# Softmax attention for one query row, forward and backward: the twelve middle head pairs load K in two pieces around V, finish dK before V's phase, and walk V by quarters of its rows

## The chip, the cores and the metric

The kernel runs on one core of a Trainium2 chip. The metric is device time in microseconds (us). A core has TensorE (PE in the profile, its weight loads PEld), VectorE (DVE), ScalarE (ACT), GpSimd (POOL) and SyncE (SP). The first four compute; SP here does nothing but issue transfers, on one queue. Matmuls write to PSUM, everything else lives in SBUF, and q, k, v and the outputs lie in HBM, which is reached by DMA: sixteen DMA engines serve the core.

## The reference

There are 32 heads, one query row each, 8192 keys and a head size of 128, all in bf16. The forward function is softmax attention, and the gradients of q, k and v are asked for too.

```python
B, H, Sq, Skv, Dh = 1, 32, 1, 8192, 128

def _fwd_reference(q, k, v):
    scale = q.shape[-1] ** -0.5
    scores = jnp.einsum('bhqd,bhkd->bhqk', q, k) * scale
    attn = _softmax(scores, axis=-1)
    return jnp.einsum('bhqk,bhkd->bhqd', attn, v)

_out, _vjp = jax.vjp(_f, q, k, v)
_grads = _vjp(grad_out)          # dq, dk, dv
```

For one head with the probabilities p, this is out = p·V, dV = p ⊗ grad_out, dp = V·grad_out, ds = p·(dp − sum(p·dp))·scale, dq = ds·K, dK = ds ⊗ q. K and V are each read once (67 MB each) and dK and dV are each written once (67 MB each). That makes 268 MB in all, and hardly any arithmetic beside it.

## The kernel before, in words

**Tiles.** Two heads make one turn t, and there are 16 turns. A turn's K is one SBUF tile of 128 partitions by 128 rows by 128 columns (4 MB; partition p holds 128 consecutive rows of the pair), and so is its V. Three K tiles and two V tiles rotate: K of turn t+2 goes into the tile of turn t−1, V of turn t+2 into that of turn t. dK and dV are written over K and V in place, eight blocks of 16 rows each, by one VectorE product per block (`outer`, L366), and stored from there (`store`, L376). So a load into a tile waits until the store out of it has landed.

**Scores.** `k_block(t, c)` (L197) transposes block c of K on VectorE (L200) into one of three buffers of the pool `XK`, and four matmuls (L208) add the block's scores into the PSUM bank `s_ps`. `s_back` transposes the bank, `s_top` finds the maximum, `s_exp` and `s_sum` give the exponentials and their sum, `p_of` (L246) gives p, four times repeated for the products, and the weights `win_p`.

**V's phase.** Three things read V before dV overwrites it. `contract(t, "p")` (L344, 32 matmuls) gives the output. dp comes from two halves in turns 3 to 14 (`wide(t)`): half of the rows go through TensorE transposes and ScalarE copies (`v_part`, L272 and L278) and `v_scores` (L289); the other half goes through VectorE transposes (`v_block`, L296, which also uses the `XK` buffers) and `v_wide` (L306). Both halves add into the bank `dp_ps`. `v_back` (L315) transposes it, `pd_sum` (L324) sums, `ds_of` (L329 to L335) gives ds, and `contract(t, "ds")` gives dq.

**Order.** The order on each engine is written out by hand: between L100 and L590 nothing is reordered, so the program's order is each engine's order. In a middle turn before the change, VectorE does five dK products of the turn before (`dk(0, 5)`), then the softmax, then the four V blocks with three more dK products spread among them, then two dV products, `v_back`, one dV product, `ds_of`, and then five dV products alternating with the K blocks 0 to 4 of the next turn, followed by K blocks 5 to 7.

**SP's queue.** It is in order: a transfer that has to wait holds those behind it. In a turn it issues the store of dK(t−1), the store of dV(t), the load of K(t+2) (waiting for the landing of the dK(t−1) store) and the load of V(t+2) (waiting for the landing of the dV(t) store).

Turns 0 to 2 and 15 use another order (`first()` and the `else` branches), with V wholly on TensorE and ScalarE. Turn 14 stores dK in two pieces, turn 15 dK and dV in four.

Of the kernel before, what the change touches and what calls it, by code (L numbers as in the profile page):

```python
# [21 lines left out]
ST = 4  # L22
K_BUFS = 3
V_BUFS = 2


@with_exitstack
def kernel(
# [49 lines left out]
    def load(x, X, t, parts):  # L78
        L = NT // parts
        for c in range(parts):  # L80
            nc.sync.dma_start(X[t][:, c * L:(c + 1) * L, :], rows_of(x, t, c * L, (c + 1) * L))
# [3 lines left out]

    def load_v(t, parts=1):
        load(v, Vt, t, parts)

    rows = consts.tile([H, 2, D], BF16)
    nc.scalar.dma_start(rows[:, 0, :], q.rearrange("b h s d -> (b h s) d"))  # L90
# [81 lines left out]
    dq_all = consts.tile([P, H], F32)  # L172

    def prepare(t):
        x = st[t] = {}
        x["m"] = psM.tile([P, 512], F32, tag="m", name="m_ps")
        for s in range(2):
            nc.tensor.matmul(x["m"][s * HF:(s + 1) * HF, 256:512],
                             lhsT=ident[0:H, 2 * t + s:2 * t + s + 1].to_broadcast([H, HF]),
                             rhs=rows[:].rearrange("h a d -> h (a d)"), start=True, stop=True, skip_group_check=True)  # L180
        x["qd"] = small.tile([P, 2, D], BF16, tag="qd", name="qd")
        nc.scalar.copy(x["qd"][:].rearrange("p a d -> p (a d)"), x["m"][:, 256:512])
# [12 lines left out]
            nc.scalar.copy(do_wide[a * QD:(a + 1) * QD, :, a * QD + SL - 1], do_four[a * QD:(a + 1) * QD, :, t])  # L195

    def k_block(t, c):  # L197
        x = st[t]
        X = xkpool.tile([P, BN, NW, QD], F32, tag="XK", name="XK_sb")
        nc.vector.transpose(X[:], Kt[t][:, c * BN:(c + 1) * BN, :].rearrange("p n d -> p (n d)").bitcast(F32).rearrange(  # L200
            "p (n w j) -> p n w j", n=BN, w=NW))
        if c == 0:
            x["s"] = psS.tile([P, 512], F32, tag="s", name="s_ps")
        cols = X[:].rearrange("p n w i -> p (n w i)").bitcast(BF16).rearrange(
            "p (n w i e) -> p w e n i", n=BN, w=NW, e=2)
        for w in range(NW):
            for e2 in range(2):
                nc.tensor.matmul(x["s"][:], lhsT=q_win[:, 2 * w + e2, SL - 1 - c:SL - 1 - c + P],  # L208
                                 rhs=cols[:, w, e2], start=(c == 0 and w == 0 and e2 == 0),
                                 stop=(c == NB - 1 and w == NW - 1 and e2 == 1), skip_group_check=True)  # L210
# [45 lines left out]
    def wide(t):  # L256
        return 3 <= t < HP - 1
# [22 lines left out]
    def v_scores(t, z):  # L280
        x = st[t]
        cols = x.pop(("XV", z)).rearrange("p m s -> p (m s)").bitcast(BF16).rearrange(
            "p (m s e) -> p e m s", s=P, e=2)
        if z == 0:
            x["dp"] = psD.tile([P, 512], F32, tag="dp", name="dp_ps")
        at = SL - 2 - 2 * z
        for e2 in range(2):
            for b in range(NQ):
                nc.tensor.matmul(x["dp"][b * QD:(b + 1) * QD, :], lhsT=do_win[:, b // 2, e2, at:at + QD],  # L289
                                 rhs=cols[:, e2, :, b * QD:(b + 1) * QD],  # L290
                                 start=(z == 0 and e2 == 0), stop=(not wide(t) and z == NZ - 1 and e2 == 1), skip_group_check=True)

    def v_block(t, r):

# [5 lines left out]
    def v_wide(t, r):  # L300
        cols = st[t].pop(("XW", r))[:].rearrange("p n w i -> p (n w i)").bitcast(BF16).rearrange(
            "p (n w i e) -> p w e n i", n=NM, w=NW, e=2)
        at = SL - 1 - (SL // 2 + r)
        for w in range(NW):
            for e2 in range(2):
                nc.tensor.matmul(st[t]["dp"][:], lhsT=do_wide[:, 2 * w + e2, at:at + P], rhs=cols[:, w, e2], start=False,  # L306
                                 stop=(r == SL // 2 - 1 and w == NW - 1 and e2 == 1), skip_group_check=True)

    def rows_in(x):
        return x.rearrange("p (m r) -> p m r", r=SL)  # L310
# [40 lines left out]
    def gather(t, which):  # L351
        S_ = backs.tile([P, 4, D], F32, tag="back", name="S_" + which)
        nc.scalar.copy(S_[:].rearrange("p j d -> p (j d)"), acc.pop(which)[:])
        bank, to = st[max(st)]["m"], (o_all if which == "p" else dq_all)
        pick = lane[:].rearrange("p (w j) -> p j w", j=4)
        at = 8 if which == "p" else 16
        for j in range(4):
            nc.tensor.matmul(bank[:, at:at + 2 * ST], lhsT=S_[:, j, :], rhs=pick[:, j, :],
                             start=(j == 0), stop=(j == 3), skip_group_check=True)
        nc.scalar.copy(to[:, 2 * (t - ST + 1):2 * (t + 1)], bank[:, at:at + 2 * ST])  # L360
# [104 lines left out]
    for t in range(1, HP + 1):  # L465
        o = t - 1
        now = t < HP
        parts = 4 if o == HP - 1 else 2 if o == HP - 2 else 1

        def dk(a, b):  # L470
            for r in range(a, b):
                outer(o, "ds", r)
                if (r + 1) % (NB // parts) == 0:
                    store(o, "ds", parts, r * parts // NB)

        blocks = now and wide(t)

        if blocks:

            dk(0, 5)  # L480
            s_back(t)
            s_top(t)
            for m in range(3):
                v_bank(t, m)
            v_block(t, 0)
            rs = s_exp(t)
            for m in range(3):
                v_copy(t, m)
            v_block(t, 1)
            v_part(t, 3)  # L490
            s_sum(t, rs)
            v_scores(t, 0)
            v_wide(t, 0)
            dk(5, 6)
            p_of(t)
            v_part(t, 4)
            v_part(t, 5)
            v_block(t, 2)
            v_wide(t, 1)
            v_part(t, 6)  # L500
            v_part(t, 7)
            v_block(t, 3)
            contract(t, "p")
            v_scores(t, 1)
            v_wide(t, 2)
            v_wide(t, 3)
            weights_do(t + 1)
            if wide(t + 1):
                weights_wide(t + 1)
        else:  # L510
            dk(0, 3)
            if now:
                v_part(t, 3)
                v_part(t, 4)
                s_back(t)
                s_top(t)
                v_scores(t, 0)
                v_part(t, 5)
                v_part(t, 6)
                rs = s_exp(t)  # L520
                for m in (7, 8, 9):
                    v_bank(t, m)
                s_sum(t, rs)
                v_copy(t, 7)
                v_copy(t, 8)
            dk(3, 4)
            if now:
                p_of(t)
                v_copy(t, 9)
                v_scores(t, 1)  # L530
                v_part(t, 10)
                v_part(t, 11)
                contract(t, "p")
                v_part(t, 12)
                v_part(t, 13)
                v_scores(t, 2)
                v_part(t, 14)
                v_part(t, 15)
                v_scores(t, 3)
                if t + 1 < HP:  # L540
                    weights_do(t + 1)
                    if wide(t + 1):
                        weights_wide(t + 1)
        if not now:
            dk(4, NB - 1)
            results()
            dk(NB - 1, NB)
            break
        dk(6 if blocks else 4, NB)
        fine = t == HP - 1  # L550
        outer(t, "p", 0)
        outer(t, "p", 1)
        if fine:
            store(t, "p", 4, 0)
        v_back(t)
        pd_sum(t)
        if t % ST == 0:
            gather(o, "ds")
        outer(t, "p", 2)
        ds_of(t)  # L560
        contract(t, "ds")
        if t % ST == ST - 1:
            gather(t, "p")
        if t + 1 < HP:
            prepare(t + 1)
        else:
            gather(t, "ds")
        for r in range(3, NB):
            outer(t, "p", r)
            if fine and r % 2:  # L570
                store(t, "p", 4, r // 2)
            if t + 1 < HP and t != 1 and r >= HALF - 1:
                k_block(t + 1, r - HALF + 1)
        if not fine:
            store(t, "p")
        if t == 1:
            for c in range(HALF + 1):
                k_block(t + 1, c)
        if t + 1 < HP:
            for c in range(HALF + 1, NB):  # L580
                k_block(t + 1, c)
                if not wide(t + 1):
                    v_part(t + 1, c - HALF - 1)
            if t + 2 < HP:
                weights_q(t + 2)
        if t + 2 < HP:
            load_k(t + 2)
            load_v(t + 2)

    order.__exit__(None, None, None)  # L590

# [29 lines left out]
```

## Time and profile before

| | |
|---|---|
| median of 3 runs | 635.58 us (635.32 to 635.61) |
| profiled execution | 635.21 us, span 633.4 us |
| moved | 268.92 MB, mean 425 GB/s |
| busy: VectorE | 558.7 us, 88% of the span |
| busy: TensorE matmuls | 426.1 us, 67% |
| busy: ScalarE | 156.9 us, 25% |
| mean granted TensorE clock | 0.83 of full speed |

The profile is one execution. Its first part gives busy time by engine, the second cuts the span into 40 slices of 15.8 us (digits are tenths; the DMA row is the mean busy share of the sixteen DMA engines), the third lists the DMA queues, the fourth follows the chain of work that ended last back from the end. The trace also answers for stretches: who waited for whom, when SP issued what, and the clock that TensorE was granted. Transfers on one queue follow one another, so a transfer's time from issue to landing holds the rest of the transfers before it.

### The profile page before, as it was taken

To read this page: it belongs to the slowest core of one execution; us is meant where nothing else is said; L and a number is where in the kernel's file an instruction comes from. 1 tells how busy PE (TensorE), PEld (TensorE's weight loads), DVE (VectorE), ACT (ScalarE), POOL (GpSimd) and SP (SyncE) were. 2 spreads that over 40 slices of the span, in tenths; PEclk is the share of its full clock that TensorE was granted. 3 is DMA by queue.
4 is the path that set the end of the run, shared out by engine and by line. 5 is a ranking of instruction groups with operands and counts; after the bars stand their busy time and mean duration, and the time that the engine had idled before them with its cause. 6 is when DMAs were issued, how large, how long until landed. Compare 5 with 4: busy or idle time off the path is not lost.

```text
span 633.4 us, 7259 instructions
## 1 busy us (share of the span) xinstructions
PE 426.1 (67%) x2876; PEld 227.8 (36%) x2876; DVE 558.7 (88%) x662; ACT 156.9 (25%) x407; POOL 9.3 (1%) x27
## 2 busy tenths in 40 slices
PE   5968686478665767457776586756758667387950
PEld 2635252243423425134352342524415243152630
DVE  7688988989989899798998979899898998989891
ACT  1616052040311304114041220412304032040610
POOL 2000000000000000000000000000000000000000
PEclk9979597887788887878878888888898788987955
DMA  8999999999999999999999999999999999999996
GB/s 364 431 429 403 447 431 429 430 428 426 436 432 434 433 430 435 429 430 427 429 430 430 432 434 435 432 435 436 426 435 431 432 429 432 426 435 429 416 422 269
DMA packets 12177, 268.92 MB, mean 425 GB/s; under 512 B 1520, under 2 KB 1520, under 8 KB 1520
## 3 DMA queue, kind: packets, MB, share of 16 engines
q1 hardware_dynamic: 12048, 268.46, 98.9%
q8 instruction: 22, 0.36, 0.2%
q14 instruction: 11, 0.09, 0.0%
q10 hardware_dynamic: 96, 0.02, 0.0%
HBM read 134.23 MB, written 134.23 MB: 424 GB/s over the span
## 4 chain that ended last, share of the span: by engine, by line
DMA 42%; DVE 30%; PE 15%; issue 7%; ACT 3%; DVEq 0%; ACTq 0%; SPq 0%
DMA out_dram<-K 22%; DMA K<-in_k_dram 18%; DVE XK_sb L200 12%; DVE K L366 10%; PE T_ps L272 6%; DVE V L366 5%; PE dp_ps L306 3%; PE s_ps L208 2%; ACT XV_sb L278 2%; PE acc_p L344 2%; PE dp_ps L289 1%; DVE sT L215 1%; DMA rows<-in_grad_out_dram 1%; PE m_ps L223 1%; PE acc_ds L344 1%
## 5 line engine op out<-in xcount | busy, mean ns | idle before, releaser
L208 PE MATMUL s_ps<-XK_sb,q_win 128*128 128x512 bf16 x512 | 149.7, 433 | 50.0 <-DVE XK_sb L200 46.8
L200 DVE STREAM_TRANSPOSE XK_sb<-K 128x1024 f32<-128x1024 f32 x128 | 152.4, 1224 | 14.4 <-DMA K<-in_k_dram 12.0
L366 DVE TENSOR_TENSOR V<-p_rep,qd 128x2048 bf16<-128x2048 bf16 x128 | 151.9, 1205 | 2.9 <-ACT K L278 2.4
L366 DVE TENSOR_TENSOR K<-ds_rep,qd 128x2048 bf16<-128x2048 bf16 x128 | 147.8, 1209 | 0.1
L208 PEld LDWEIGHTS <-q_win 128*128 128x128 bf16 x512 | 53.7, 107 | 139.1 <-issue 103.7
L272 PE MATMUL T_ps<-ident_f,V 128*128 128x128 f32 x640 | 102.4, 320 | 0.1
L272 PEld LDWEIGHTS T_ps<-ident_f,V 128*128 128x128 f32 x640 | 91.7, 167 | 14.2 <-issue 2.2
L278 ACT COPY XV_sb<-T_ps 128x512 f32<-128x512 f32 x144 | 78.5, 587 | 69.5 <-PE T_ps L272 69.3
L344 PE MATMUL acc_ds<-K,win_ds 128*32 128x512 bf16 x512 | 50.7, 566 | 28.8 <-ACT win_ds L244 27.3
L296 DVE STREAM_TRANSPOSE XV_blk<-V 128x1024 f32<-128x1024 f32 x48 | 59.6, 1241 | 7.7 <-PE dp_ps L306 7.4
L223 PE MATMUL m_ps<-ident_f,top 128*128 128x128 f32 x16 | 6.5, 405 | 71.9 <-DVE top L222 71.9
L306 PE MATMUL dp_ps<-XV_blk,do_wide 128*128 128x512 bf16 x192 | 49.2, 387 | 0.0
L185 ACT COPY q_win<-q_blk 128x16 bf16<-128x16 bf16 x16 | 4.2, 261 | 159.8 <-PE s_ps L208 159.8
L344 PEld LDWEIGHTS <-win_ds 128*32 128x32 bf16 x512 | 16.3, 126 | 50.5 <-ACT win_ds L244 27.0
L344 PE MATMUL acc_p<-V,win_p 128*32 128x512 bf16 x512 | 30.9, 380 | 1.5 <-ACT win_p L244 1.5
L223 PEld LDWEIGHTS m_ps<-ident_f,top 128*128 128x128 f32 x16 | 2.6, 164 | 78.4 <-issue 73.2
L289 PE MATMUL dp_ps<-XV_sb,do_win 128*32 128x512 bf16 x288 | 24.1, 412 | 8.3 <-ACT XV_sb L278 8.1
L233 ACT ACTIVATE e<-sT,nbias 128x128 f32<-128x128 f32 x16 | 8.3, 520 | 80.7 <-DVE nbias L230 80.7
L306 PEld LDWEIGHTS <-do_wide 128*128 128x128 bf16 x192 | 16.9, 98 | 27.5 <-issue 13.0
L315 DVE STREAM_TRANSPOSE dpT<-dp_ps 128x512 f32<-128x512 f32 x16 | 11.5, 717 | 13.6 <-PE dp_ps L306 12.3
L324 PE MATMUL m_ps<-pd,same 128*128 128x1 f32 x32 | 6.3, 267 | 19.6 <-DVE m_ps L318 19.6
L344 PEld LDWEIGHTS <-win_p 128*32 128x32 bf16 x512 | 12.4, 96 | 14.4 <-issue 4.6
(68 smaller groups left out, 206.7 us busy)
## 6 DMA issues: line engine op xcount, KB each, us to landing
K<-in_k_dram SPq DMA_DIRECT2D x15, 4096.0 KB, 19.3
V<-in_v_dram SPq DMA_DIRECT2D x14, 4096.0 KB, 19.3
out_dram<-K SPq DMA_DIRECT2D x14, 4096.0 KB, 28.2
out_dram<-V SPq DMA_DIRECT2D x14, 4096.0 KB, 20.2
V<-in_v_dram SPq DMA_DIRECT2D x8, 1024.0 KB, 11.3
out_dram<-V SPq DMA_DIRECT2D x8, 1024.0 KB, 19.2
K<-in_k_dram SPq DMA_DIRECT2D x4, 1024.0 KB, 8.0
out_dram<-K SPq DMA_DIRECT2D x2, 2048.0 KB, 13.8
```

What stands on the lines that cost most here:

```text
L200: nc.vector.transpose(X[:], Kt[t][:, c * BN:(c + 1) * BN, :].rearrange("p n d -> p (n d)").bitcast(F32).rearrange("p (n w j) -> p n w j", ...
L208: nc.tensor.matmul(x["s"][:], lhsT=q_win[:, 2 * w + e2, SL - 1 - c:SL - 1 - c + P], rhs=cols[:, w, e2], start=(c == 0 and w == 0 and e2 == 0),
L223: nc.tensor.transpose(x["m"][:, 128:256], top[:].to_broadcast([P, P]), ident_f[:])
L233: nc.scalar.activation(e[:].rearrange("p (c n) -> p n c", c=NB), x["sT"][:, :, 0:NB], ACT.Exp, bias=nbias[:], scale=scale, accum_out=rs[:])
L272: nc.tensor.transpose(T_ps[:, j, :], words[:, at * P:(at + 1) * P], ident_f[:])
L278: nc.scalar.copy(x["XV", z][:, i * TB:(i + 1) * TB, :], x.pop(("T", m))[:])
L289: nc.tensor.matmul(x["dp"][b * QD:(b + 1) * QD, :], lhsT=do_win[:, b // 2, e2, at:at + QD], rhs=cols[:, e2, :, b * QD:(b + 1) * QD], start ...
L296: nc.vector.transpose(X[:], Vt[t][:].rearrange("p n d -> p (n d)").bitcast(F32).rearrange("p (m r w j) -> p m r w j", r=SL, w=NW, j=QD)[:, ...
L306: nc.tensor.matmul(st[t]["dp"][:], lhsT=do_wide[:, 2 * w + e2, at:at + P], rhs=cols[:, w, e2], start=False, stop=(r == SL // 2 - 1 and w = ...
L315: nc.vector.transpose(dpT[:].rearrange("p m r -> p (m r)"), x.pop("dp")[:])
L344: nc.tensor.matmul(acc[which][b * QD:(b + 1) * QD, :], lhsT=win[which][:, g, at:at + QD], rhs=X[:, 4 * g:4 * g + 4, :].rearrange("p n d -> ...
L366: nc.vector.tensor_tensor(X[:, a:b, :].rearrange("p n (a b) -> p n a b", b=R), x[which][:, a:b, :].unsqueeze(2).to_broadcast([P, BN, D // ...
```

## The change

It acts on turns 3 to 14, the ones in which `wide(t)` holds.

- **Loads.** `load_pair` loads the first five of K's eight blocks (`NA = 5`), then V, then the last three blocks of K, as three transfers instead of two. It waits for the same landings as before.
- **K blocks.** Blocks 0 and 1 of turn t+1 come before `v_back(t)`; blocks 2 to 4 at the end of turn t, after the last dV product; blocks 5 to 7 at the start of turn t+1, ahead of the dK products. `weights_q` goes with them.
- **dK.** All eight dK products of turn t−1 come before V's phase: four ahead of `s_back`, one between `s_top` and `s_exp`, three between `s_sum` and `p_of`.
- **V.** Three V blocks are transposed first. Then four quarters follow, each with one `v_wide`, eight matmuls of `contract(t, "p")`, two `v_part`, and the two dV products that overwrite that quarter's rows (blocks 0 to 5 in the first three quarters). `v_scores` comes at the end, the K blocks 0 and 1 of the next turn behind it, then `v_back`; dV products 6 and 7 stand on either side of `ds_of`.
- **dp's bank.** The first `v_wide` opens the sum, the last `v_scores` closes it.

```diff
+    def load_pair(t):
+        cut = NA * BN if wide(t) else NT
+        nc.sync.dma_start(Kt[t][:, 0:cut, :], rows_of(k, t, 0, cut))
+        load_v(t)
+        if cut < NT:
+            nc.sync.dma_start(Kt[t][:, cut:NT, :], rows_of(k, t, cut, NT))
...
         if blocks:
-            dk(0, 5)
+            for c in range(NA, NB):
+                k_block(t, c)
+            weights_q(t + 1)
+            dk(0, 4)
             s_back(t)
             s_top(t)
-            for m in range(3):
-                v_bank(t, m)
-            v_block(t, 0)
+            dk(4, 5)
             rs = s_exp(t)
...
             s_sum(t, rs)
-            v_scores(t, 0)
-            v_wide(t, 0)
-            dk(5, 6)
+            dk(5, NB)
             p_of(t)
...
+            for r in range(3):
+                v_block(t, r)
+            for i in range(4):
+                v_wide(t, i)
+                if i == 0:
+                    v_block(t, 3)
+                contract(t, "p", i * NG // 4, (i + 1) * NG // 4)
+                for z in range(2):
+                    v_part(t, z * (NM // TB) + i)
+                if i < 3:
+                    outer(t, "p", 2 * i)
+                    outer(t, "p", 2 * i + 1)
+            for z in range(2):
+                v_scores(t, z)
             weights_do(t + 1)
             if wide(t + 1):
                 weights_wide(t + 1)
+            k_block(t + 1, 0)
+            k_block(t + 1, 1)
+            early = NB - 2
...
-        dk(6 if blocks else 4, NB)
+        if not blocks:
+            dk(4, NB)
+            outer(t, "p", 0)
+            outer(t, "p", 1)
...
         v_back(t)
         pd_sum(t)
...
-        outer(t, "p", 2)
+        outer(t, "p", early)
         ds_of(t)
         contract(t, "ds")
...
-        for r in range(3, NB):
+        done = 2 if blocks else 0
+        for r in range(early + 1, NB):
             outer(t, "p", r)
...
         if t + 1 < HP:
-            for c in range(HALF + 1, NB):
+            for c in range(done, NA if wide(t + 1) else NB):
                 k_block(t + 1, c)
...
         if t + 2 < HP:
-            load_k(t + 2)
-            load_v(t + 2)
+            load_pair(t + 2)
```

The loads of turns 3 to 14 are issued at the ends of turns 1 to 12. Turn 15 still loads its K whole, but two of its K blocks are asked for in the middle of turn 14.

More of the change, by code (lines that the diff above doesn't have):

```diff
@@ L24 @@
 V_BUFS = 2
+NA = 5
 @with_exitstack
@@ L174, in prepare @@
     def prepare(t):
-        x = st[t] = {}
+        x = st.setdefault(t, {})
         x["m"] = psM.tile([P, 512], F32, tag="m", name="m_ps")
@@ L197, in k_block @@
     def k_block(t, c):
-        x = st[t]
+        x = st.setdefault(t, {})
         X = xkpool.tile([P, BN, NW, QD], F32, tag="XK", name="XK_sb")
@@ L283, in v_scores @@
             "p (m s e) -> p e m s", s=P, e=2)
-        if z == 0:
+        if z == 0 and not wide(t):
             x["dp"] = psD.tile([P, 512], F32, tag="dp", name="dp_ps")
@@ L290, in v_scores @@
                                  rhs=cols[:, e2, :, b * QD:(b + 1) * QD],
-                                 start=(z == 0 and e2 == 0), stop=(not wide(t) and z == NZ - 1 and e2 == 1), skip_group_check=True)
+                                 start=(not wide(t) and z == 0 and e2 == 0),
+                                 stop=(z == (1 if wide(t) else NZ - 1) and e2 == 1), skip_group_check=True)
     def v_block(t, r):
@@ L303, in v_wide @@
         at = SL - 1 - (SL // 2 + r)
+        if r == 0:
+            st[t]["dp"] = psD.tile([P, 512], F32, tag="dp", name="dp_ps")
         for w in range(NW):
             for e2 in range(2):
-                nc.tensor.matmul(st[t]["dp"][:], lhsT=do_wide[:, 2 * w + e2, at:at + P], rhs=cols[:, w, e2], start=False,
-                                 stop=(r == SL // 2 - 1 and w == NW - 1 and e2 == 1), skip_group_check=True)
+                nc.tensor.matmul(st[t]["dp"][:], lhsT=do_wide[:, 2 * w + e2, at:at + P], rhs=cols[:, w, e2],
+                                 start=(r == 0 and w == 0 and e2 == 0), stop=False, skip_group_check=True)
     def rows_in(x):
@@ L353, in gather @@
         nc.scalar.copy(S_[:].rearrange("p j d -> p (j d)"), acc.pop(which)[:])
-        bank, to = st[max(st)]["m"], (o_all if which == "p" else dq_all)
+        bank, to = st[max(u for u in st if "m" in st[u])]["m"], (o_all if which == "p" else dq_all)
         pick = lane[:].rearrange("p (w j) -> p j w", j=4)
@@ L478 @@
         if blocks:
-            dk(0, 5)
+            for c in range(NA, NB):
+                k_block(t, c)
+            weights_q(t + 1)
+            dk(0, 4)
             s_back(t)
             s_top(t)
-            for m in range(3):
-                v_bank(t, m)
-            v_block(t, 0)
+            dk(4, 5)
             rs = s_exp(t)
[L487 to L490, printed above, removed]
             s_sum(t, rs)
-            v_scores(t, 0)
-            v_wide(t, 0)
-            dk(5, 6)
+            dk(5, NB)
             p_of(t)
[L496 to L506, printed above, removed]
+            for r in range(3):
[12 more added lines that the diff above has]
+                v_scores(t, z)
             weights_do(t + 1)
@@ L509 @@
                 weights_wide(t + 1)
+            k_block(t + 1, 0)
+            k_block(t + 1, 1)
+            early = NB - 2
         else:
+            early = 2
             dk(0, 3)
@@ L548 @@
             break
-        dk(6 if blocks else 4, NB)
         fine = t == HP - 1
[L551 to L554, printed above, removed]
+        if not blocks:
+            dk(4, NB)
+            outer(t, "p", 0)
+            outer(t, "p", 1)
+            if fine:
+                store(t, "p", 4, 0)
         v_back(t)
@@ L571 @@
                 store(t, "p", 4, r // 2)
-            if t + 1 < HP and t != 1 and r >= HALF - 1:
-                k_block(t + 1, r - HALF + 1)
+            if not blocks and t + 1 < HP and t != 1:
+                k_block(t + 1, done)
+                done += 1
         if not fine:
             store(t, "p")
-        if t == 1:
-            for c in range(HALF + 1):
+        if t + 1 < HP:
+            for c in range(done, NA if wide(t + 1) else NB):
                 k_block(t + 1, c)
-        if t + 1 < HP:
-            for c in range(HALF + 1, NB):
-                k_block(t + 1, c)
-                if not wide(t + 1):
+                if not wide(t + 1) and c > HALF:
                     v_part(t + 1, c - HALF - 1)
-            if t + 2 < HP:
+            if t + 2 < HP and not wide(t + 1):
                 weights_q(t + 2)
         if t + 2 < HP:
-            load_k(t + 2)
-            load_v(t + 2)
+            load_pair(t + 2)
     order.__exit__(None, None, None)
```

## The prediction, made before the run

> **What bounds the kernel now.** I read the page first: the slices, the queue, the chain.
>
> ```profile
> DMA  8999999999999999999999999999999999999996
> GB/s 364 431 429 403 447 431 429 430 428 426 436 432 434 433 430 435 429 430 427 429 430 430 432 434 435 432 435 436 426 435 431 432 429 432 426 435 429 416 422 269
> ...
> q1 hardware_dynamic: 12048, 268.46, 98.9%
> ...
> DMA 42%; DVE 30%; PE 15%; issue 7%; ACT 3%; DVEq 0%; ACTq 0%; SPq 0%
> ```
>
> The DMA engines are full in 38 of 40 slices; SP's one queue fills 98.9% of their span. The chain, though, gives DVE 30% and PE 15%. It runs through whatever came last at each step, and in a kernel where engines wait for loads and stores wait for engines it can go round either way. So I ask SP when it issued (a middle stretch; start, duration, transfer):
>
> ```profile
> 229.92 0.34 SPq L376 DMA_DIRECT2D out_dram<-V  x1
> 241.73 0.34 SPq L81 DMA_DIRECT2D K<-in_k_dram  x1
> 251.40 0.34 SPq L81 DMA_DIRECT2D V<-in_v_dram  x1
> 251.79 0.42 SPq L376 DMA_DIRECT2D out_dram<-K  x1
> 270.18 0.34 SPq L376 DMA_DIRECT2D out_dram<-V  x1
> 280.45 0.34 SPq L81 DMA_DIRECT2D K<-in_k_dram  x1
> 290.11 0.34 SPq L81 DMA_DIRECT2D V<-in_v_dram  x1
> ```
>
> The K load goes out when the dK store has landed (280.45), the V load when the dV store has (290.11): 9.66 us apart, one 4 MB transfer. The dV store was issued at 270.18, and its turn came at 280.45, 10.3 us later. The dK store waited for nothing but the V load ahead of it on SP. Always at least one transfer lies behind the running one: the queue, not VectorE, sets the pace. The first and last of twelve such K loads were issued at 123.33 and 553.13, so a turn takes 429.8/11 = 39.07 us; four transfers of 4.194 MB at 432 GB/s (below) are 38.84.
>
> VectorE's margin is read from its waits in 100 to 560 us (us, times, longest), about 11.8 turns:
>
> ```profile
> DVE dpT L315 <- PE dp_ps L306: 11.3, 11, 1.4
> DVE XK_sb L200 <- DMA K<-in_k_dram: 11.0, 10, 2.5
> DVE XV_blk L296 <- PE dp_ps L306: 6.6, 11, 1.6
> DVE rinv L249 <- PE m_ps L238: 3.3, 9, 0.4
> ```
>
> VectorE waits 11.0 us for K, 1.0 a turn: it is held by the queue. Without that its own turn would be about 38.1.
>
> **The change, part by part.** The profiled execution took 635.21 us, 1.8 beyond its span of 633.4 and 0.37 below the median 635.58. I add to it and put the same difference on the median.
>
> *Bytes and pieces.* The bytes are the same. Twelve K loads become two transfers each. What a cut costs shows where loads of 1 MB run (5 to 19 us) beside 4 MB ones (245 to 550 us):
>
> ```profile
> DMA packets 858, 5.94 MB, mean 424 GB/s; under 512 B 134, under 2 KB 134, under 8 KB 134
> ...
> DMA packets 4534, 131.69 MB, mean 432 GB/s; under 512 B 506, under 2 KB 506, under 8 KB 506
> ```
>
> 4.194 MB take 9.89 us in four pieces and 9.71 in one: 0.06 us a cut, twelve cuts 0.7 us. Both stretches are full, so this is on the path. The lower end is 0 (the difference may be the two small row loads in the first stretch). The upper end is the row load that stood alone, 8 KB in 3.3 us from issue to landing: twelve of those are 40 us. But the added piece is issued right behind V's load, with up to 9.7 us of bytes before it, as the 1 MB pieces were; I take 0.7.
>
> The Trainium skill (DMA: Bandwidth & Descriptors, Latency and other measured facts) gives about 0.6 us to the first byte on this kind of queue. Paid twelve times this would be 7.2 us, 643.5 in place of 636.3; the rows above show it hidden behind a queued transfer, at 0.06.
>
> *SP's order.* The load of K's first part waits for the same landing as before, V's load too, and the third piece for none. While V's load waits for the dV store's landing, only 5/8 of a K load, 6.1 us, is left in the queue where 9.7 was. SP spends 0.34 us on an issue, so nothing runs dry: 0. Behind V's load stand the third piece and the dK store; the queue still holds 9.7 us of V when they are issued. Cost 0.
>
> *Landings.* With the dV store landing at 251.4, K's first part lands at 257.5 (was 261.0), V at 267.2 (was 270.8), K's last part at 270.8. Blocks 5 to 7 now open a turn, so the wait for K moves there: VectorE starts a turn at 270.8 at the earliest.
>
> *VectorE's turn.* The same operations as before, none added: 425.6 us busy in 95 to 560 us, 35.8 a turn, and small gaps of 0.4 (39.07 less 35.8 less 34.8/11.8 of waits, two smaller ones included). Now the walk, with 1.15 us for a K block and 1.13 for a product back to back, 1.2 for a V block. From the start: three K blocks 3.5, four products 4.5, back and maximum 1.2, a product 1.1, the bias 0.45 (TensorE's transpose of the maximum took 0.45 and has 1.1), three products 3.4 that cover exponential, sum and so `rinv` (0.3 us a turn gone), `p` 0.45: V's phase starts at 14.6. Four V blocks last to 19.5. `v_wide(0)` can start once the first is there, at 15.9. A quarter on TensorE is four wide matmuls, eight of `contract` and eight transposes: 0.88 + 0.48 + 0.87 = 2.2 us at full clock, 1.82 + 0.90 + 1.71 = 4.4 at half, from the groups of four and eight in the chain (288.8 to 290.5 full, 364.6 to 368.2 half) and a quarter of 32 contractions (1.91 and 3.60). VectorE's two products per quarter take 2.3. So at full clock it never waits; at half it does. How long V's phase is at half clock now (columns: stretch, its length, TensorE busy, clock, DMA share, GB/s; transposes begin at 320.6 in one turn, 359.3 in the other):
>
> ```profile
> 320.00:322.00 2.00, 1.67 (x8) 0.50 0.87 377
> 322.00:324.00 2.00, 2.00 (x12) 0.50 0.95 410
> 324.00:326.00 2.00, 1.44 (x14) 0.99 1.22 524
> ...
> 360.00:362.00 2.00, 2.00 (x11) 0.50 0.91 393
> 362.00:364.00 2.00, 1.54 (x13) 0.50 0.95 410
> 364.00:366.00 2.00, 2.00 (x12) 0.50 1.18 508
> 366.00:368.00 2.00, 2.00 (x11) 0.50 0.87 377
> 368.00:370.00 2.00, 2.00 (x13) 0.90 0.99 426
> ```
>
> About 3.5 us in one, 8.9 in the other. With 3.5 the first quarter is through 0.4 us after the last V block, and nothing waits after that. With 8.9 the products wait 0.8 and 2.2. Then two K blocks cover `v_scores`, so the 1.0 wait before `dpT` goes; `pd_sum`, now behind eight score matmuls on TensorE, ends about when product 6 does: 0. After product 7 the K blocks run six in a row at 1.15, while TensorE needs 1.03 for one at full clock; at half (1.7), behind 3.6 of `contract`, it would hold VectorE by up to 2.4 through the three buffers. VectorE's turn: 36.2 + 0.4 = 36.6 at best, 36.2 + 3.0 = 39.2 with the long half clock, 41.6 with both. The mix seen now gives something near 38, below 39.07: hidden behind the queue, with the dV store issued 33 us into the turn (19.5 + six products 6.8 + two K blocks 2.3 + `v_back` 1.2 + two products 2.3 + `ds_of` 0.9), so near 303.8 where its place in the queue comes at 319.2: 15 ahead, where it was 10.
>
> The Trainium skill (TensorE: Matmul & The Clock Gate, Part 1) states that about 3.4 us of sustained work free the clock; by that every turn would be the 36.6 one. The 360 us rows disagree: fully busy, and at half for 8.9.
>
> *The end.* K of turn 15 lands as before plus 0.7, and turn 14 asks for two of its blocks where VectorE has two dV products left rather than five: from 573.5 two K blocks, `v_back`, two products, `ds_of`, six K blocks are 14.4 to 16.5, so dK(14) begins near 588 to 590 against 586.4. The last store piece was issued at 620.99 of 633.4; less 2.5 for its bytes and 3.3 for latency, it had 6.6 us to spare. 1.5 to 3.6 later costs 0. If that cover were gone, it would be paid in full.
>
> Sum: 635.21 + 0.7 = 635.9 for a profiled execution, 636.3 on the median.
>
> **The rivals.**
>
> *TensorE's clock makes VectorE the bound.* For it: V's phase now follows some 11 us with almost no TensorE work, and every dV product waits on that quarter. Against it: V's phase begins at half clock now as well. It decides when the mean turn is over 39.07 + 6.6/11 = 39.7. With 41.6 in every turn: 11 × 2.5 − 6.6 = 21, so 657; with a mean of 40.5, 9 more: 645.
>
> *The added transfers are not hidden.* If each stalls the queue by 0.3 to 0.6 us, 12 × 0.3 = 3.6 to 7.2: 639 to 643. It needs gaps in the queue that the 1 MB pieces do not show.
>
> *Faster.* If the 0.23 us by which a turn exceeds four transfers (39.07 against 38.84) is VectorE being late, the earlier dK and dV products win it back: 12 × 0.23 = 2.8, less 0.7, gives 633.5. It decides if any slice is short for want of an issue; the ten us to spare speak against it, and the 22 instruction fetches on these engines explain the rest better. More is not to be had from a full queue.
>
> **How the numbers follow.** My forecast 0.65, with its own range 635.5 to 637.2 (cuts between 0 and twice their price); the clock 0.20; transfers not hidden 0.09; faster 0.06. The range 635.4 to 641 holds the forecast but for 0.03, a third of the clock's cases and two thirds of the transfers': 0.75 to 0.8. Within 0.2% (1.27 us, about what a measurement here can tell from no change) lies the forecast but for a tenth above 636.85: 0.58. Slower: 0.20 + 0.09 + 0.07 and a little: 0.37; faster 0.05.
>
> **What the profile after would show.** Right: DMA full in the same slices, K's first-part loads 39.1 us apart, the K wait moved to the last part's blocks, dV stores issued about 15 us ahead of need, no `rinv` wait, waits of V's products on `T_ps` below 3 us a turn. Wrong: DMA slices below 9 in the middle, K loads over 39.7 apart, VectorE's waits on `T_ps` or `s_ps` above 3.5 a turn (the clock), or short slices just after V's loads (the pieces).

## The result and the profile after

The changed kernel took 636.56 us (median; 635.56 to 638.34) beside 635.33 us (635.07 to 635.61) for the kernel before: a ratio of 1.0017 [1.0009, 1.0024], 1.23 us slower. That is just within the 0.2% that the prediction called no change, and 0.3 us from its 636.3. The profiled execution took 636.0 us with a span of 634.2, 0.8 more than before's. One thing is new at first sight: the times of the kernel before lie within 0.5 us, those of the changed kernel are spread over 2.8.

The page of the changed kernel, the DMA rows of the 40 slices, the queue and the head of the chain:

```profile
DMA  8999999999999999999999999999999999999997
GB/s 362 432 429 400 447 422 432 437 428 429 427 432 435 435 415 425 433 433 421 412 429 431 430 428 437 434 432 428 426 426 432 429 427 430 431 430 429 422 424 320
...
q1 hardware_dynamic: 13776, 268.46, 99.3%
...
DVE 40%; PE 25%; DMA 24%; issue 5%; ACT 3%; DVEq 0%; SPq 0%; ACTq 0%
```

The DMA engines are as full as before, and SP's queue takes even more of their span (99.3% for 98.9). But full is no longer the same as fast. Slices 6, 15, 19 and 20 moved 422, 415, 421 and 412 GB/s with their digit at 9; before, no slice between the fifth and the last three was under 426. The chain now gives DVE 40% and DMA 24%, where it gave 30 and 42. That looks as if VectorE had become the bound; the experiments show that it has not.

When SP issued, in the same stretch as before (start, duration, transfer; L93 is K's first part, L96 its last):

```profile
241.11 0.34 SPq L93 DMA_DIRECT2D K<-in_k_dram  x1
250.78 0.34 SPq L82 DMA_DIRECT2D V<-in_v_dram  x1
251.17 0.43 SPq L96 DMA_DIRECT2D K<-in_k_dram  x1
251.70 0.38 SPq L388 DMA_DIRECT2D out_dram<-K  x1
265.16 0.35 SPq L388 DMA_DIRECT2D out_dram<-V  x1
280.43 0.34 SPq L93 DMA_DIRECT2D K<-in_k_dram  x1
```

The dV store goes out at 265.16 and its turn in the queue comes at 280.43: 15.3 us ahead of need, where the prediction had 15 and before had 10.3. So the queue does not want for an issue here. Yet the twelve K loads, issued from 123.01 to 554.40, are 39.22 us apart, where before's were 39.07: 11 × 0.15 = 1.65 us over the middle turns.

VectorE's waits between 100 and 560 us (us, times, longest):

```profile
DVE V L378 <- PE T_ps L281: 13.8, 17, 1.1
DVE XK_sb L209 <- PE s_ps L217: 10.5, 9, 2.6
DVE XK_sb L209 <- DMA K<-in_k_dram: 6.0, 4, 2.1
```

The waits before `dpT` and `rinv` are gone and the products of V wait for TensorE's transposes instead, 13.8 us or 1.2 a turn. The second line must not be taken at its word throughout. VectorE's timeline over two turns, with the page's row on K's last parts (the median of the us from issue to landing stands at its end) behind it:

```profile
231.80 3.50 DVE L209 STREAM_TRANSPOSE XK_sb<-K 128x1024 f32<-128x1024 f32 x3 [1.35 <-PE s_ps L217]
235.22 4.59 DVE L378 TENSOR_TENSOR K<-ds_rep,qd 128x2048 bf16<-128x2048 bf16 x4
...
246.48 4.62 DVE L306 STREAM_TRANSPOSE XV_blk<-V 128x1024 f32<-128x1024 f32 x4
251.55 7.18 DVE L378 TENSOR_TENSOR V<-p_rep,qd 128x2048 bf16<-128x2048 bf16 x6 [0.45 <-PE T_ps L281]
...
265.05 3.49 DVE L209 STREAM_TRANSPOSE XK_sb<-K 128x1024 f32<-128x1024 f32 x3
270.78 3.50 DVE L209 STREAM_TRANSPOSE XK_sb<-K 128x1024 f32<-128x1024 f32 x3 [2.23 <-PE s_ps L217]
...
291.18 2.36 DVE L378 TENSOR_TENSOR V<-p_rep,qd 128x2048 bf16<-128x2048 bf16 x2 [1.11 <-PE T_ps L281]
293.87 4.80 DVE L378 TENSOR_TENSOR V<-p_rep,qd 128x2048 bf16<-128x2048 bf16 x4 [0.33 <-PE T_ps L281]
```

```profile
K<-in_k_dram SPq DMA_DIRECT2D x12, 1536.0 KB, 19.2
```

K's last part was issued at 251.17, and 19.2 later is 270.4; the trace's record of this landing says 270.65, and block 5 started at 270.78. This wait of 2.23 us, put down to PE, ended when the load landed, and so did the one of 1.35. Two others, of 2.43 and 2.63 us in other turns, did not: there the load had landed 1.3 and 1.0 us earlier, and TensorE's score matmuls, behind `contract(t, "ds")`, released the buffer last. The other five of the nine waits are TensorE's too, 1.8 us in all. So VectorE waits some 12 us for K, 1.0 a turn as before: it is still held by the queue.

The order came out as the prediction walked it. The turn starts at 231.80, V's phase 14.68 us into it (14.6 was predicted), the dV store 33.4 into it (33).

Last, where the bytes were short: two stretches of the same place in neighbouring turns (start and end, length, busy us of PE, PEld, DVE, ACT and POOL with their counts, PEclk, DMA share, GB/s).

```profile
304.00:309.00 5.00, 4.57 (x42) 2.93 (x42) 4.48 (x4) 0.87 (x3) 0.00 (x0) 0.62 1.06 392
344.00:349.00 5.00, 3.53 (x37) 1.23 (x37) 4.57 (x7) 0.76 (x3) 0.00 (x0) 0.72 1.05 446
```

Both are full. In the first, while K's last part is moved, the engines bring 392 GB/s, in the second 446. In the trace's packet records a packet of that part has 12 KB and normally takes an engine 460 ns; in 5 of the 12 turns 13 to 46 of the 128 packets take clearly longer, up to 1.1 us. The engines are busy all that time (without a packet for 0.04 us of 100 to 560, as a mean of the sixteen), so no view of busy shares shows it.

### The profile page after: what moved, and what is told of

Its sections match the earlier page's. It is cut to its first block, busy times and chain, and to the rows that moved or that the text cites. A ratio compares the mean times of both kernels' runs of the same rounds, so it can differ in the third digit from the quotient of the medians.

```text
span 634.2 us, 7269 instructions
## 1 busy us (share of the span) xinstructions
PE 420.3 (66%) x2876; PEld 207.0 (33%) x2876; DVE 561.6 (89%) x662; ACT 159.3 (25%) x407; POOL 9.3 (1%) x27
## 3 DMA queue, kind: packets, MB, share of 16 engines
q1 hardware_dynamic: 13776, 268.46, 99.3%
## 4 chain that ended last, share of the span: by engine, by line
DVE 40%; PE 25%; DMA 24%; issue 5%; ACT 3%; DVEq 0%; SPq 0%; ACTq 0%
DVE K L378 15%; DMA K<-in_k_dram 13%; DMA out_dram<-V 11%; DVE XK_sb L209 9%; DVE V L378 8%; PE T_ps L281 6%; PE dp_ps L318 5%; PE s_ps L217 4%; PE acc_p L356 4%; PE acc_ds L356 3%; DVE XV_blk L306 1%; DVE sT L224 1%; ACT XV_sb L287 1%; PE dp_ps L298 1%; DVE dpT L327 1%
## 5 line engine op out<-in xcount | busy, mean ns | idle before, releaser
L217 PE MATMUL s_ps<-XK_sb,q_win 128*128 128x512 bf16 x512 | 132.5, 401 | 14.7 <-DVE XK_sb L209 11.8
L281 PE MATMUL T_ps<-ident_f,V 128*128 128x128 f32 x640 | 94.8, 298 | 0.1
L318 PE MATMUL dp_ps<-XV_blk,do_wide 128*128 128x512 bf16 x192 | 61.9, 451 | 49.7 <-DVE XV_blk L306 49.7
L281 PEld LDWEIGHTS T_ps<-ident_f,V 128*128 128x128 f32 x640 | 77.3, 152 | 34.2 <-issue 26.2
L217 PEld LDWEIGHTS <-q_win 128*128 128x128 bf16 x512 | 49.6, 101 | 90.0 <-issue 44.9
L306 DVE STREAM_TRANSPOSE XV_blk<-V 128x1024 f32<-128x1024 f32 x48 | 55.4, 1212 | 0.0
L356 PE MATMUL acc_p<-V,win_p 128*32 128x512 bf16 x512 | 42.7, 428 | 1.5 <-ACT win_p L253 1.5
L298 PE MATMUL dp_ps<-XV_sb,do_win 128*32 128x512 bf16 x288 | 20.9, 385 | 5.1 <-ACT XV_sb L287 5.0
L260 ACT ACTIVATE p_rep<-e,rinv 128x512 bf16<-128x512 f32 x16 | 11.6, 726 | 39.4 <-DVE rinv L258 39.4
L247 PE MATMUL m_ps<-rs,same 128*128 128x1 f32 x32 | 8.3, 329 | 18.8 <-ACT e L242 18.8
## 6 DMA issues: line engine op xcount, KB each, us to landing
K<-in_k_dram SPq DMA_DIRECT2D x12, 1536.0 KB, 19.2
```

The source lines that it names most:

```text
L247: nc.tensor.matmul(st[t]["m"][:, 0:1], lhsT=same[:], rhs=rs[:], start=True, stop=True, skip_group_check=True)
L260: nc.scalar.activation(x["p"][:], x["e"][:].unsqueeze(2).to_broadcast([P, NT, R]), ACT.Copy, scale=rinv[:])
L281: nc.tensor.transpose(T_ps[:, j, :], words[:, at * P:(at + 1) * P], ident_f[:])
L306: nc.vector.transpose(X[:], Vt[t][:].rearrange("p n d -> p (n d)").bitcast(F32).rearrange("p (m r w j) -> p m r w j", r=SL, w=NW, j=QD)[:, ...
L356: nc.tensor.matmul(acc[which][b * QD:(b + 1) * QD, :], lhsT=win[which][:, g, at:at + QD], rhs=X[:, 4 * g:4 * g + 4, :].rearrange("p n d -> ...
```

## The experiments

The theory behind the first four runs is that the 1.23 us are a sum: the new order, the cuts of K's load, and the place of its last part. Each difference below is to the kernel before on the same chip (635.25 us for the first four, 635.41 for w_minus2, w_plus3, a_na3 and a_vcut, 635.45 for the last four); the ratio has its 95% interval.

### The parts of the change

**a_whole**: the changed kernel with K loaded whole.

```diff
-        cut = NA * BN if wide(t) else NT
+        cut = NT
```

> The changed order of work, but K of every turn loaded in one transfer ahead of V. Theory (the queue is the bound and the cuts cost): the loss goes, 635.3 to 635.6 beside 635.3 before and 636.6 changed. Rival (the new order on VectorE and TensorE costs the 1.2 us, by the clock or by the later end of turn 14): it stays at 636.3 to 636.8, or gets worse, since K's first blocks land 3.6 us later in a turn. VectorE should now wait for K ahead of blocks 0 of the next turn, in the middle of a turn, and not ahead of block 5.

Measured: 634.2 us (634.02 to 634.5), 0.9981 [0.9973, 0.999]. The new order alone gains 1.05 us. The time is under both expectations, and the prediction had this term at nothing. This is the fastest of all the kernels here that compute the whole, ahead of both the one before and the one after.

**a_adjacent**: two pieces, both ahead of V.

```diff
         nc.sync.dma_start(Kt[t][:, 0:cut, :], rows_of(k, t, 0, cut))
-        load_v(t)
         if cut < NT:
             nc.sync.dma_start(Kt[t][:, cut:NT, :], rows_of(k, t, cut, NT))
+        load_v(t)
```

> The changed kernel with both pieces of K ahead of V: the same twelve cuts, no piece of K between V's load and the dK store. If a cut costs by itself (0.06 us each): 636.0, and packets of the second piece take as long as their bytes say. If the loss lies in the place of the last piece, just ahead of the store: 635.3 to 635.6. If it lies in the order of work: 636.6.

Measured: 634.85 us (634.61 to 635.17), 0.9994 [0.9986, 1.0003]. That is below all three expected values, because they were counted without the gain of the order. Against a_whole the twelve cuts cost 0.65 us (the slowest run of a_whole is faster than the fastest of this kernel); the prediction's term was 0.7. Against the changed kernel (+1.23 here, −0.40 there) the place of the last part between V's load and the dK store costs 1.63.

So the change is −1.05 + 0.65 + 1.63 = +1.23 us. The third term is what the first two leave, and the sizes hold for the parts taken in this sequence: the changed kernel's own interval reaches from about +0.6 to +1.5.

**b_cut** and **b_between** make the same two steps from the other side. They leave the order of before as it is and change the loads alone; `load_pair` is that of the change, and in b_cut its last two transfers change places.

```diff
-            load_k(t + 2)
-            load_v(t + 2)
+            load_pair(t + 2)     # b_cut: both pieces of K ahead of V
                                  # b_between: V between them, as in the change
```

> The kernel before, with K of turns 3 to 14 in two pieces, both ahead of V: the cuts alone. Theory: 635.3 + 12 x 0.06 = 636.0. If a cut is free: 635.3. If the order of work is what costs: 635.3.

> The kernel before, with the changed kernel's three transfers (K's first part, V, K's last part) and its own order of work: the loads alone. Theory: 636.0 to 636.6, the whole loss, and the slow packets of the last piece here too. Rival (order of work): 635.3. VectorE asks for block 5 at about the time when the last part lands, so it should lose less than 1 us a turn to it, hidden by the queue.

Measured: b_cut 638.45 us (638.32 to 638.62), 1.0051 [1.0038, 1.0064]; b_between 640.26 us (637.43 to 644.61), 1.0092 [1.0062, 1.0121]. By the medians the place costs 1.8 us in the old order too, but the six times are spread over 7.2 us, and the lowest is under b_cut's: the size is loose. The cuts cost 3.2 there, five times what they cost in the new order, which no expectation covers, and b_between is outside its expectations with them. Taken in this sequence the same change is 3.2 + 1.8 − 3.8: the parts do not simply add, and the order is worth more where the loads are cut. K loads are 39.32 us apart in b_cut and 39.11 in a_adjacent; 11 × 0.21 = 2.3 us of the difference arise there. Its cause stays open.

### Does VectorE or the queue set the end?

**w_minus2** takes two products out of each turn of a_whole (dV blocks 2 and 4 of turns 3 to 14 are not computed), **w_plus3** adds three transposes to each.

```diff
     def outer(t, which, r):
+        if wide(t) and which == "p" and r in (2, 4):      # w_minus2
+            return
```

```diff
-        nc.vector.transpose(X[:], ...)
+        for _ in range(2 if wide(t) and c in (2, 3, 4) else 1):      # w_plus3
+            nc.vector.transpose(X[:], ...)
```

> The changed order with K whole, and dV's blocks 2 and 4 of turns 3 to 14 not computed (V's rows are stored there), 2.3 us less on VectorE in a turn. Theory (the queue is the bound): unchanged, 634.0 to 634.5, VectorE waits 2.3 more a turn for K. Rival (VectorE and TensorE share the bound): up to 12 x 2.3 = 27 less, any gain over 1 us speaks for it.

> The changed order with K whole, and K blocks 2, 3 and 4 of turns 3 to 14 transposed twice into the same buffer, 3 x 1.15 = 3.5 us more on VectorE in a turn. Theory: VectorE's own turn is 39.07 less 1.3 of waits for K = 37.8, so 41.3 with this, 2.2 over the queue's: about 12 x 2.2 = 26 less the 6.6 us of room at the end, 20 more: 654 (640 to 660). If VectorE has far more room than I think: 634 to 636; if it has none: 634 + 12 x 3.5 = 676.

Measured: w_minus2 634.2 us (633.98 to 634.34), 0.998 [0.9971, 0.9989], the same as a_whole; w_plus3 653.0 us (651.02 to 653.62), 1.0271 [1.0257, 1.0285].

VectorE's waits between 100 and 560 us in a_whole:

```profile
DVE V L378 <- PE T_ps L281: 14.2, 17, 1.1
DVE XK_sb L209 <- DMA K<-in_k_dram: 11.6, 10, 2.2
DVE XK_sb L209 <- PE s_ps L217: 3.7, 5, 1.8
```

in w_minus2:

```profile
DVE V L380 <- PE T_ps L281: 27.7, 33, 1.2
DVE XK_sb L209 <- DMA K<-in_k_dram: 20.3, 10, 3.6
DVE XK_sb L209 <- PE s_ps L217: 4.5, 8, 1.8
```

and in w_plus3, all that is listed:

```profile
DVE V L379 <- PE T_ps L282: 9.7, 12, 1.1
DVE pdt L342 <- ACT dq_all L373: 1.6, 3, 0.5
```

Less work on VectorE turns into longer waits, and the time stays: the queue is the bound of a_whole, whose order is the changed kernel's. With three more transposes every wait for K is gone, and VectorE paces the kernel: the step from scores to softmax comes at 125.28 us in turn 3 and at 576.99 in turn 14, 41.06 us a turn. Less three transposes of 1.16 its own turn is 37.6, against the queue's 39.08. Over twelve turns 42 us of work were added and 18.6 paid (17.6 over the kernel before, where a_whole is 1.05 under it). The margin is real, and it speaks against a bound behind the 40% of the chain that go to VectorE in the changed kernel.

### Why is the place dear?

**a_na3** and **a_vcut** test whether the last part suffers because it is short, a 1.5 MB piece of 12 KB packets between two 4 MB transfers. a_na3 makes it the longer one (three blocks first, five behind V); turn 2's loop then stops at the third K block. a_vcut keeps K whole and gives the short piece at that place to V.

```diff
-NA = 5
+NA = 3                                                    # a_na3
...
-            if not blocks and t + 1 < HP and t != 1:
+            if not blocks and t + 1 < HP and t != 1 and done < (NA if wide(t + 1) else NB):
```

```diff
-        load_v(t)
-        if cut < NT:
-            nc.sync.dma_start(Kt[t][:, cut:NT, :], rows_of(k, t, cut, NT))
+        at = NA * BN if wide(t) else NT                   # a_vcut, cut = NT
+        nc.sync.dma_start(Vt[t][:, 0:at, :], rows_of(v, t, 0, at))
+        if at < NT:
+            nc.sync.dma_start(Vt[t][:, at:NT, :], rows_of(v, t, at, NT))
```

> The changed kernel with K cut at three blocks instead of five: the piece between V's load and the dK store is 2.5 MB, 6.1 us of bytes per DMA engine, not 1.5 MB and 3.6. Theory short (packets are slow there because the piece is shorter than the engines are apart, 3 to 5 us, so that one engine still loads V while another already stores dK): the slow packets go, 634.7 to 635.2, as with both pieces ahead of V. Theory address (a K load next to a dK store in the queue is slow, whatever its length): they stay, 636 to 638 with a spread. VectorE does five K blocks at the start of a turn in place of three; the queue hides it.

> The changed order of work with K whole and V cut at five blocks: the short piece just ahead of the dK store is V's. Theory short: slow packets in it, 636 to 638. Theory address (K beside dK): none, 634.2 + 12 x 0.06 = 634.9.

Measured: a_na3 660.97 us (659.41 to 662.28), 1.041 [1.0396, 1.0425]; a_vcut 634.92 us (634.8 to 635.78), 0.9992 [0.9983, 1.0001]. Both refute it, and a_na3 is far outside its other expectation as well. The longer piece at that place costs 25.6 us, and a short piece of V there costs nothing beyond its cuts (0.56 us over a_whole). Three stretches of one turn of a_na3, columns as above, the second of them within K's last part; and the DMA's own row for 110 to 550 us:

```profile
344.00:356.90 12.90, 11.19 (x96) 6.13 (x98) 12.15 (x16) 5.93 (x17) 0.31 (x1) 0.99 1.00 409
356.90:360.00 3.10, 3.10 (x32) 0.98 (x24) 1.84 (x2) 0.00 (x0) 0.00 (x0) 0.50 0.97 320
360.00:372.00 12.00, 7.24 (x30) 2.65 (x26) 9.10 (x9) 0.63 (x2) 0.00 (x0) 0.86 1.01 433
```

```profile
DMA packets 7721, 179.39 MB, mean 408 GB/s; under 512 B 863, under 2 KB 863, under 8 KB 863
```

At a share of 0.97 the engines bring 320 GB/s: here the slowing is in every turn. Most packets of 20 KB take 761 ns, but 362 of the 1536 take over 1.0 us, up to 2.5. K loads are 41.31 us apart.

**n_adjacent, n_fromv, n_swap** take a_na3 apart: both pieces ahead of V; the last part read from the rows of v in place of k; the outputs of dK and dV exchanged.

```diff
-        load_v(t)                                         # n_adjacent
         if cut < NT:
             nc.sync.dma_start(Kt[t][:, cut:NT, :], rows_of(k, t, cut, NT))
+        load_v(t)
```

```diff
-            nc.sync.dma_start(Kt[t][:, cut:NT, :], rows_of(k, t, cut, NT))
+            nc.sync.dma_start(Kt[t][:, cut:NT, :], rows_of(v, t, cut, NT))     # n_fromv
```

```diff
-        X, dst = (Kt[t], out_2) if which == "ds" else (Vt[t], out_3)
+        X, dst = (Kt[t], out_3) if which == "ds" else (Vt[t], out_2)           # n_swap
```

> The same kernel with both pieces of K (three and five blocks) ahead of V. Theory (the place of K's last piece makes the 661, not the five K blocks at the start of a turn): 634.7 to 635.2. Rival (the order of work): 655 to 661.

> The kernel with K cut at three blocks and V between (661), but its last piece of K is read from the same rows of v in HBM instead of k, so K's blocks 3 to 7 hold V's data; queue, sizes, SBUF tiles and instructions are the same. Theory address in HBM (reading k while the dK output is written is what is slow): the slow packets go, 634.7 to 636. Rival (the place in the queue or the SBUF tiles): 659 to 662.

> The same kernel (K cut at three blocks, V between, 661) with the two outputs exchanged: dK goes to the output of dV and dV to that of dK. The last piece of K then runs beside writes to the other output. Theory of one pair (k and the dK output lie badly to each other in HBM): 634.7 to 636, or a loss elsewhere, where K's first part follows the dV store. Theory of any write beside a piece of k, or of SBUF: 659 to 662.

Measured: n_adjacent 635.44 us (634.87 to 637.09), 1.0004 [0.9995, 1.0013]; n_fromv 659.72 us (658.59 to 661.15), 1.0379 [1.0363, 1.0395]; n_swap 661.78 us (659.74 to 663.17), 1.0415 [1.0396, 1.0434]. The place makes the 25.6 us, whole: with the same pieces and the same order of work, the kernel with both ahead of V is at −0.01. Five K blocks at the start of a turn are no burden. Neither the rows that the part is read from nor the tensor that the next store is written to makes the difference.

The place changes one thing more, which the views of busy shares hide. V's load is issued only when the last engine has landed the dV store, and until then the engines that are ahead live on the transfer between, K's first part: a whole K tile in before and a_whole, both pieces in a_adjacent and n_adjacent, but three blocks, 3.6 us of bytes at 432 GB/s, in a_na3. SP in one of its turns:

```profile
166.66 0.34 SPq L93 DMA_DIRECT2D K<-in_k_dram  x1
176.30 0.34 SPq L82 DMA_DIRECT2D V<-in_v_dram  x1
```

Counted from the packet records, about six of the sixteen engines have no packet under way from 176 to 178 us. After each V load issued between 100 and 560 us, 5 to 13 engines run dry at the worst point. As a mean of the sixteen, engines are without a packet for 5.4 us of that stretch in a_na3, 8.0 in n_fromv, 8.9 in n_swap, 0.8 in b_between, 0.04 in the changed kernel (five blocks, 6.1 us), and at most 0.01 in all the kernels with a whole K tile ahead of V but one. The one is w_plus3, 2.3 us, where the stores come late from VectorE. It has slow packets as well, 310 of 5883 of 32 KB against 35 of 6045 in a_whole, and its page shows full slices of 388 to 402 GB/s with no piece of K anywhere:

```profile
DMA  8999999999999999999999999999999999999798
GB/s 363 439 428 397 440 434 430 439 425 436 425 432 434 429 438 425 428 423 408 429 400 392 419 401 434 421 388 418 411 424 397 412 395 410 426 419 402 312 376 367
```

So the 25.6 us are in part a queue that runs dry on single engines, and for the rest packets that take longer. That the slow packets follow from the dry engines is not shown, since the changed kernel has them with hardly any dry time. Two things were not varied: how many bytes stand ahead of V's load with no piece behind it, and the tile that is written while its neighbour is read.

### Where does the new order gain?

In a_whole the fifteenth K load is issued at 553.10 us, in the kernel before at 553.13. The middle turns run alike, and the gain lies in the last 80 us (79.3 for 80.3). VectorE's work there hardly explains it: SP issues the last store piece 0.80 us earlier than before in a_whole (620.19 for 620.99), but 0.67 later in a_adjacent, whose span ends 0.3 earlier too. One theory was that instruction fetches, which run on the same DMA engines, put one engine behind the others, and that the order decides when. **b_pad** adds 24 small matmuls to each of turns 3 to 6 of the kernel before, so that the fetches move and the work hardly does.

```diff
+            if 3 <= t < 7:
+                for _ in range(24):
+                    nc.tensor.matmul(st[t + 1]["m"][:, 2:3], lhsT=ident[:], rhs=ident[:, 0:1], start=True, stop=True, ...)
```

> The kernel before with 24 matmuls of one column in an unused column of a PSUM bank at the end of turns 3 to 6, where TensorE is idle: 192 instructions more, so the later instruction fetches fall at other points and in other turns. Theory (the slowest DMA engine ends the run, and which fetches it carries decides 1 us): the time moves by 0.3 to 1.2 us either way from 635.4. Rival (the order of work itself wins the 1.1 us of the changed order with whole loads): unchanged within 0.2.

Measured: 635.83 us (635.5 to 636.91), 1.0009 [1.0, 1.0018]. A shift of 0.38 us, inside the theory's range and with an interval that touches none: this decides nothing. Where the 1.05 us come from is open.

## Why the prediction was right, and where it was not

The total was right, 636.56 for 636.3. The working was half right: of the three terms of the change, one was sized well and two were put at nothing that are +1.63 and −1.05 us, and these two largely cancel. That the total came out so close is luck; the sum was not close.

- *The queue is the bound*: right, and shown by w_minus2 and w_plus3.
- *Cuts, 0.7*: right, 0.65 in a_adjacent and 0.56 in a_vcut. By the 0.6 us to the first byte that the prediction quoted from the Trainium skill (DMA: Bandwidth & Descriptors, Latency and other measured facts), twelve would be 7.2; the runs show 0.05 for each behind a queued transfer. But b_cut, with 3.2 us, shows that the price does not hold in every order; the 1 MB pieces of one stretch were too narrow a ground for it.
- *SP's order, cost 0*: this step failed. It asked whether the queue runs dry, and in the changed kernel it does not. It took for granted that a full queue moves its bytes at one rate wherever a piece stands in it. The place between V's load and the dK store costs 1.63 us. With the cut at three blocks it costs 25.6, and there the step fails in its own terms too, because engines do run dry while V's load waits. Of the prediction's signs of being wrong, short slices about V's loads came true, in GB/s and not in the digits. The 0.09 for the rival of transfers that are not hidden had this in it, though with an empty queue as the reason, and in the changed kernel the queue was full.
- *More is not to be had from a full queue*: failed for the order. a_whole gains 1.05 us, in the last 80 us and not by the rival's 0.23 a turn: its K loads are 39.08 apart, before's 39.07. *The end, 0* is the term that was off, by −1.05, and the runs do not show why. Its claim that a later store costs nothing stands: a_adjacent issued its last store piece 0.67 us later than the kernel before and still ended earlier.
- *Landings and VectorE's turn*: right in nearly every number. V's phase was predicted at 14.6 and began at 14.68, the dV store at 33 and was at 33.4, 15 ahead of need and 15.3 was measured; the K wait moved to block 5; the `dpT` and `rinv` waits went. In two turns TensorE held VectorE through the three buffers after `contract`, with the 2.4 us that the prediction gave as the most (2.43 and 2.63, of which 1.3 and 1.0 came after the landing of K). VectorE's own turn was put near 38, and w_plus3 gives 37.6.
- *The range*: twice the price of the cuts gives 637.0 as its upper end, not 637.2; nothing hangs on it.
- *TensorE's clock makes VectorE the bound (0.20)*: fell. The mean granted clock between 95 and 560 us is 0.80, 0.83 before, but V's products wait 1.2 us a turn, not 3. The first product waited 0.45 us in one turn (0.4 was predicted for 3.5 us of half clock) and 1.11 and 0.33 in the next (0.8 and 2.2 for 8.9 us). By the trace's clock records V's phase begins at half clock in all twelve turns and stays there for 4.1 to 6.7 us, where the transposes of before had 2.9 to 9.1. The prediction called its rows about 360 us fully busy; one of the four rows at 0.50 has TensorE at 1.54 of 2.00 us.

## What to carry to other kernels

Where a queue is the bound, ask of a moved transfer not only whether the queue stays full but what it moves when it is full: read GB/s beside the busy share, slice by slice, since 320 and 446 GB/s both show as full. Where a load waits for a store to land, ask how many bytes lie between the two in the queue: with three blocks of K there, single engines ran dry in every turn of a_na3. Test the bound by taking compute away and adding some before you trust the chain of waits, which gave 40% to an engine with 1.5 us a turn to spare. And when a change has several parts, run the parts alone even if the total comes out as forecast: here the order without the cuts (634.2 us) beats both kernels.

## What was not expected of the hardware

- The same number of bytes in the same queue takes 25.6 us longer (660.97 against 635.44, each against the kernel before on its chip) when 2.5 MB of K stand between V's load and dK's store instead of ahead of V, at a busy share near 1. With 1.5 MB there it is 1.6 us, and some 1.8 in the old order, unevenly from execution to execution. With 1.5 MB of V there it is nothing beyond the cuts. Shortness, the rows that are read, the output that is written next and the order of work are ruled out by runs. Single engines run dry in the slow kernels, 5.4 us of 460 as a mean in a_na3; for the slow packets, the larger part, no cause is shown.
- A cut of a load costs 0.05 us in one order of work (a_adjacent, a_vcut) and 0.27 in another (b_cut); a_adjacent and b_cut have the same transfers in the same order on the queue.
- Two orders of work whose queues run alike to 553 us end 1 us apart (a_whole and the kernel before).
